# A spectral filter gated with a Mish layer: idle matmuls on a built-in f32 constant, and a weight load cut in two with a table between

## The chip, the cores and the metric

The kernel runs on one core of a Trainium2 chip. The metric is device time in microseconds (us). Before the change the median of three runs is 135.92 us (135.65 to 135.99). Engines are named as in the profile: PE (matmul) with PEld (its weight loads), DVE, ACT, POOL, and SP, which issues most DMAs.

## What is computed

Two branches work on arrays of 2048 rows of 512, in bf16, and a gate for each row mixes them. Branch A filters `x` in the 2-D Fourier domain; branch B is a layer with Mish and a second layer; both take the same `x` (`A_x`).

```python
g = sigmoid((x * gate_w).sum(-1, keepdims=True))          # x = A_x, [1, 2048, 512]
X = rfft2(x.astype(float32)) * (A_w_r + 1j * A_w_i)       # weights [2048, 257]
a = irfft2(X, s=(2048, 512)).astype(bfloat16)
h = einsum("bsd,df->bsf", x, B_w1) + B_b1                 # 512 -> 1792
b = einsum("bsf,fd->bsd", h * tanh(softplus(h)), B_w2)    # 1792 -> 512
return g * a + (1 - g) * b
```

## The kernel before

The rows are 16 tiles of 128 (`t`), in four chunks of four tiles (`c`). Everything is on one core, and PE does nearly all of it: both Fourier transforms are matmuls with tables of cosines and sines that the program holds as constants in DRAM.

**Branch B.** `x` is transposed on PE tile by tile (L516, with a permutation `pid` that POOL builds) and copied to `xT`. Layer 1 (L575, `layer1`) is, for a chunk and for each of 14 blocks `ft` of 128 columns of `w1`, four matmuls of 128x512 into one PSUM bank; ACT applies Mish with the bias (L560). Layer 2 (L903, L886) is 14 matmuls for each tile, scaled by one minus the gate at eviction.

**Branch A.** The transform along a row (L609 to L612, `a1`, with the table `FDs`), the transform along the columns in two steps (L630 and L745) with a trip through DRAM between, the filter on DVE and POOL (L756, L762), the way back (L798, a second trip through DRAM, L828 and L846), and the mix.

**The head.** The first chunk is taken in halves, so that PE can begin with part of the loads. Tiles 0 and 2 (`b`=0) and 1 and 3 (`b`=1) come in two loads of `x` (`ld_x0`), and the first 512 columns of `w1` in four loads, one for each block `dt_` of 128 input rows (`ld_w1d`). PE transposes tiles 0 and 2 (eight transposes, `tr0d0` to `tr0d3`); then `early0` to `early3` (L590) multiply them with one `ld_w1d` piece each, four matmuls of 256 columns, one for each of four output blocks; after `early0` come the eight transposes of tiles 1 and 3 (`tr1d*`). `late0` to `late3` (L590, four matmuls each) do the second half of the four blocks. The rest of chunk 0 (`mm1_0_4` on, L575) needs further loads of `w1`: `ld_w1(4, 8)` for blocks 4 to 7, `ld_w1(8, 14)` for the others. The row transforms need `FDs` (`ld_fd`).

**Idle matmuls.** Until the first load has landed, PE multiplies a tile of zeros with itself (`warm`, L504; `zt` is set by DVE at L500). The one piece of real work in between is the transpose of the bias (`tr_small`, L519). Their number is set by the planner.

**What sets the order.** The order on every engine is written by a planner when the program is built (`_Graph.schedule`, L215). Each task has an engine, a duration, dependencies and a priority. The planner walks through time, takes the ready task that can start first (within 0.1 us the one of highest priority), and books its duration. DMAs have an estimated bandwidth `bw`, from which the planner books when they land (L287 to L295); loads on one queue stay in the order in which they are written down. Idle matmuls are *fillers* of priority 1, which are dropped as soon as `early0` has been placed (L239). On the chip each engine runs its list in that order and waits on semaphores; the planner's times do not reach the chip, only the order.

SP's list begins: `x0` first half, `w1d0`, `x0` second half, `w1d1`, `w1d2`, `w1d3`, `w1` 4 to 7, `FDs`, `x` of chunk 1, `w1` 8 to 13, the table `m1`, `x` of chunks 2 and 3, and smaller ones. POOL issues the filter's weights and `w2` when `w1` 8 to 13 has landed.

Of the kernel before, what the change touches and what calls it, by code (L numbers as in the profile page):

```python
# [7 lines left out]
BF = mybir.dt.bfloat16  # L8
F32 = mybir.dt.float32
AF = mybir.ActivationFunctionType  # L10
# [20 lines left out]
def _bf16_bits(a):  # L31
    a = np.ascontiguousarray(a, dtype=np.float32)
    u = a.view(np.uint32)
    r = (u + np.uint32(0x7FFF) + ((u >> np.uint32(16)) & np.uint32(1))) >> np.uint32(16)
    return r.astype(np.uint16)
# [280 lines left out]
def _build(nc, A_x, A_w_r, A_w_i, B_x, B_w1, B_b1, B_w2, gate_w, out):  # L316
    cs = _build_consts()
    d_FD = nc.inline_tensor(_bf16_bits(cs["FD"]), name="c_fd").bitcast(BF)
# [7 lines left out]
    G = _Graph()  # L326
    es = ExitStack()
    with es:
        def sb(name, shape, dt):
            return es.enter_context(nc.sbuf_tensor(name, shape, dt))  # L330

        xo = sb("xo", [128, NT, 512], BF)
# [4 lines left out]
        act = sb("act", [128, 3, NFT, 512], BF)  # L337
        w1_sb = sb("w1_sb", [128, 4, F], BF)
        w2_sb = sb("w2_sb", [128, NFT, 512], BF)
        FDs = sb("FDs", [128, 768], BF)  # L340
# [6 lines left out]
        Ybuf = sb("Ybuf", [128, 32 * KR], BF)  # L347
        junk = sb("junk", [128, 512], BF)
        gwb = sb("gwb", [128, 512], BF)
        zt = sb("zt", [128, 256], BF)  # L350
        braw = sb("braw", [14, 128], BF)
        b1f = sb("b1f", [128, NFT], F32)
        gdot = sb("gdot", [128, NT], F32)
# [12 lines left out]
        q1 = sb("q1", [128, 2, 2, 16], F32)  # L366
# [25 lines left out]
        ps = es.enter_context(nc.psum_tensor("ps", [128, 8, 512], F32))  # L392
        psb = ps.bitcast(BF)

        xv = A_x[0].rearrange("(s p b) d -> p s b d", s=2, b=8)
        ov = out[0].rearrange("(s p b) d -> p s b d", s=2, b=8)
        w1v = B_w1.rearrange("(dt p) f -> p dt f", p=128)
# [7 lines left out]
        def new_sem(name):  # L405
            return es.enter_context(nc.semaphore(name))
# [5 lines left out]
        def dma(name, dst, src, reads=(), writes=(), nbytes=0, deps=(), is_out=False, prio=None, queue="sp", bw=300e3):  # L412
            dur = 1.0 if queue == "pool" else 0.5

            def fn(e, _dst=dst, _src=src):
                return e.dma_start(_dst, _src)

            t = G.add(name, queue, dur, fn, reads=reads, writes=writes, lat=2.0 + nbytes / bw, deps=deps, prio=prio)
            t.xfer = nbytes / bw
            t.isdma = True  # L420
            if is_out:
                t.sem = out_sem
                n_out_dma[0] += 1
                t.semval = 16 * n_out_dma[0]
            else:
                t.sem = new_sem("d_" + name)
                t.semval = 16
            return t
# [16 lines left out]
        def evict(name, n, dst, src, reads, writes, prio=None, rate=1.0):  # L445
# [9 lines left out]
              reads=["ones"], writes=["perm"])  # L455
        G.add("id14", "pool", 0.2, lambda e: e.affine_select(out=id14[:, :], in_=id14[:, :], pattern=[[1, 14]],
                                                             compare_op=ALU.is_equal, fill=0.0, base=0, channel_multiplier=-1),
              reads=["ones"], writes=["id14"])

        def ld_x(c, s0, s1):  # L460
            dma(f"ld_x{c}{s0}", xo[:, 4 * c + 2 * s0:4 * c + 2 * s1, :].rearrange("p (s b) d -> p s b d", b=2), xv[:, s0:s1, 2 * c:2 * c + 2, :],
                writes=[("x", t) for t in range(4 * c + 2 * s0, 4 * c + 2 * s1)], nbytes=128 * 2048 * (s1 - s0), bw=330e3 if c == 1 else 380e3)

        def ld_x0(b):
            dma(f"ld_x0{b}", xo[:, b:4:2, :], xv[:, :, b, :], writes=[("x", b), ("x", 2 + b)], nbytes=128 * 2048, bw=(218e3, 350e3)[b])

        def ld_w1d(dt_):
            dma(f"ld_w1d{dt_}", w1_sb[:, dt_, 0:512], w1v[:, dt_, 0:512], writes=[("w1d", dt_)], nbytes=128 * 1024, bw=350e3)

        def ld_w1(lo, hi):  # L470
            return dma(f"ld_w1_{lo}", w1_sb[:, :, 128 * lo:128 * hi], w1v[:, :, 128 * lo:128 * hi],
                       writes=[("w1", f) for f in range(lo, hi)], nbytes=512 * 256 * (hi - lo), bw=220e3 if lo == 4 else 380e3)

        dma("ld_b1", braw[:, :], B_b1.rearrange("(ft p) -> ft p", p=128), writes=["braw"], nbytes=3584, queue="act", prio=100.0)
        ld_x0(0)
        ld_w1d(0)
        ld_x0(1)
        for dt_ in range(1, 4):
            ld_w1d(dt_)
        ld_w1(4, 8)  # L480
        dma("ld_fd", FDs[:], d_FD[:], writes=["FD"], nbytes=128 * 1536, bw=262e3)
        ld_x(1, 0, 2)
        t_w1 = ld_w1(8, 14)
        dma("ld_m1", m1g1[:, 0:2048], d_M1.rearrange("p b h c m -> p (b h c m)"), writes=["m1"], nbytes=128 * 4096)
        ld_x(2, 0, 2)
# [4 lines left out]
        for i in range(2):  # L490
            for q in (0, 2, 1, 3):
                dma(f"ld_W{i}{q}", WT[32 * q:32 * q + 32, i, :, :].rearrange("p g k -> p (g k)"), Wv[i][q],
                    writes=[("W", i, q)], nbytes=32 * 8224, queue="pool", deps=[t_w1])
        WALL = [("W", i, q) for i in range(2) for q in range(4)]
        for h in range(2):
            dma(f"ld_w2_{h}", w2_sb[:, 7 * h:7 * (h + 1), :], w2v[:, 7 * h:7 * (h + 1), :],
                writes=[("w2", h)], nbytes=128 * 7 * 1024, queue="pool", deps=[t_w1])


        G.add("zero", "dve", 0.15, lambda e: e.memset(zt[:, :], 0.0), writes=["zt"], prio=99.0)  # L500
        G.add("table", "act", 1.5, lambda e: e.activation(q1[:, 0, 0, 0:1], zt[:, 0:1], AF.Mish), reads=["zt"], prio=99.0)
        for i in range(NWARM):
            n_ = 256 if i < 15 else 128
            G.add(f"warm{i}", "pe", n_ / 1200, lambda e, n_=n_: e.matmul(ps[:, 6, 0:n_], zt[:, 0:128], zt[:, 0:n_], start=True, stop=True),  # L504
               reads=["zt"], prio=1.0).filler = True


        SP0 = PR['sp0']
# [2 lines left out]
        def f_tr(e, ts, dts, at):  # L511
# [8 lines left out]
           reads=["braw", "id14"], writes=[("bank", 0)], prio=SP0 + 4.0)  # L520
        G.add("ev_small", "act", 0.25, lambda e: e.activation(b1f[:, :], psb[:, 0, 0:14], AF.Copy), reads=[("bank", 0)], writes=["b1f"], prio=SP0 + 1.05)
        for b in range(2):
            for dt_ in range(4):
                bk = (dt_ + 1) % 4
                pe(f"tr{b}d{dt_}", 2 * mm((256, 128)[b]), lambda e, dt_=dt_, bk=bk, b=b: f_tr(e, (b, 2 + b), (dt_,), lambda t, d_: (bk, t // 2)),
                   reads=[("x", b), ("x", 2 + b), "perm"], writes=[("bank", bk)], prio=SP0 + 1.0 + 2.5 * b - 0.01 * dt_)
# [3 lines left out]
                      reads=[("bank", bk)], writes=[("xT", t, dt_) for t in (b, 2 + b)], prio=SP0 + 1.1)  # L530

        for c in range(NCH):
            for t in range(4 * c, 4 * c + 4):
                if c > 0:
                    pe(f"tr{t}", 4 * mm(128), lambda e, t=t: f_tr(e, (t,), range(4), lambda t, dt_: (1, dt_)), reads=[("x", t), "perm"],
                       writes=[("bank", 1)], prio=SP0 + 1.0)
# [7 lines left out]
            for h, op in ((0, ALU.add), (1, ALU.subtract)):  # L544
# [3 lines left out]
                lo, hi = uv[:, 0:2, r2, :], uv[:, 2:4, r2, :]  # L548
# [45 lines left out]
        for dt_ in range(4):  # L594
            t_e = pe(f"early{dt_}", 4 * mm(256) * (1.8 if dt_ == 0 else 1), lambda e, dt_=dt_: f_early(e, range(4), (dt_,), 0), writes=[("bank", b) for b in EB],
                     reads=[("xT", 0, dt_), ("xT", 2, dt_), ("w1d", dt_)], prio=PR['mm1c0'] + 8)
            if dt_ == 0:
                G.filled = t_e
        for ft in range(4):
            pe(f"late{ft}", 4 * mm(256), lambda e, ft=ft: f_early(e, (ft,), range(4), 1), writes=[("bank", EB[ft])],  # L600
               reads=[("xT", t, dt_) for t in (1, 3) for dt_ in range(4)] + [("w1d", dt_) for dt_ in range(4)], prio=PR['mm1c0'] + 7 - 0.01 * ft)
            mish(0, ft, EB[ft])

        for t in range(NT):
            a1b = t % 2 if t >= 8 else 0

            def f_a1(e, t=t, a1b=a1b):
# [9 lines left out]
               writes=[("bank", a1b)], prio=SP0)  # L617
# [4 lines left out]
            if t % 4 == 3:  # L622
# [17 lines left out]
                for h in range(2):  # L640
                    t_r1w.append(dma(f"r1w{t}_{h}", scr1_w[h][:, b0:b0 + 8, :], Y1[64 * h:64 * h + 64, b0:b0 + 8, :],
                                     reads=[("Y1", b0 + i) for i in range(8)], writes=[("scr1", b0 + i, h) for i in range(8)],
                                     nbytes=64 * 8 * 512, prio=SP0 + 1.0, bw=180e3))
# [3 lines left out]
        for t in range(NT):  # L647
# [3 lines left out]
                  reads=[("x", t), "gw"], writes=[("gd", t), "junk"], deps=s1_tasks[2:3])  # L651
# [37 lines left out]
        for n in range(4):  # L689
            t_r1r.append(dma(f"r1r{n}", In2[:, :, 2 * n:2 * n + 2, :].rearrange("p q u k -> p q (u k)"), scr1_r[:, :, 512 * n:512 * n + 512],  # L690
                             reads=[("scr1", b, h) for b in range(32) for h in range(2)],
                             writes=[("In2", q, u) for q in range(4) for u in (2 * n, 2 * n + 1)],
# [43 lines left out]
        for n in range(4):  # L736
            zb = n % 2

            def f_s2(e, n=n):
                ins = None  # L740
                for c in range(2):
                    for q in range(4):
                        for h in range(2):
# [6 lines left out]
                               reads=[("In2", q, 2 * n + uu) for q in range(4) for uu in range(2)] + ["sm"], writes=BSB))  # L750
            for i in range(4):
                h, uu = divmod(i, 2)
                u, pb = 2 * (2 * n + uu) + h, uu
                for (nm, Pb, Wu) in (("1", P1b, WT[:, :, u, 0:256]), ("2", P2b, WT[:, ::-1, u, 0:256])):
# [5 lines left out]
                          reads=[("bank", 2 * h), ("bank", 2 * h + 1)] + WALL, writes=[("P" + nm, pb)])  # L760
                for (c, nm, Pb, op) in ((0, "1", P1b, ALU.subtract), (1, "2", P2b, ALU.add)):
# [3 lines left out]
                                reads=[("P" + nm, pb)], writes=[("Z", zb, i, c)])  # L765
                if n == 0 and i == 1:
                    s2_tasks.append(pe("s2x", 0.8, f_s2x, reads=[("In2", q, u_) for q in range(4) for u_ in range(8)] + ["sm", "rr"],
                                       writes=[("bank", 0), ("bank", 1)]))
# [4 lines left out]
                          reads=["q"], writes=["zr"])  # L773
                    G.add("zi", "pool", 0.15, lambda e: e.tensor_tensor(out=zi[:], in0=q2[:, 0], in1=q2[:, 1], op=ALU.add),
                          reads=["q"], writes=["zi"])
                    G.add("z0r", "pool", 0.15, lambda e: e.tensor_tensor(out=z0[:, 0, :], in0=zr[:, 0, :], in1=zi[:, 1, :], op=ALU.subtract),
                          reads=["zr", "zi"], writes=["z0r"])
                    G.add("z0i", "pool", 0.15, lambda e: e.tensor_tensor(out=z0[:, 1, :], in0=zi[:, 0, :], in1=zr[:, 1, :], op=ALU.add),
                          reads=["zr", "zi"], writes=["z0i"])
            if n == 0:  # L780
                G.add("gexp", "pool", 2.9, lambda e: e.tensor_tensor(out=gexp[:, :], in0=gbase[:, :], in1=gdot[:, :], op=ALU.pow),  # L781
                      reads=[("gd", t) for t in range(NT)] + ["gbase"], writes=["gexp"])
                G.add("gden", "pool", 0.2, lambda e: e.tensor_scalar(out=gexp[:, :], in0=gexp[:, :], scalar1=1.0, scalar2=None, op0=ALU.add),
                      reads=["gexp"], writes=["gden"])
                G.add("gcol", "dve", 0.2, lambda e: e.reciprocal(out=gcol[:, :], in_=gexp[:, :]), reads=["gden"], writes=["gcol"])
                G.add("omg", "dve", 0.1, lambda e: e.tensor_scalar(out=omg[:, :], in0=gcol[:, :], scalar1=-1.0, scalar2=1.0, op0=ALU.mult, op1=ALU.add),
                      reads=["gcol"], writes=["omg"])
            G.add(f"wc_{n}", "pool", 0.2, lambda e, n=n, zb=zb: e.tensor_copy(
                out=Zb[:, zb, :, :, :, 0], in_=z0[:].rearrange("p c (u h) -> p h c u", h=2)[:, :, :, 2 * n:2 * n + 2]),
                reads=["z0r", "z0i"], writes=[("Z", zb, 4)])  # L790

            def f_s2i(e, zb=zb):
# [10 lines left out]
               writes=BSB)  # L803
# [3 lines left out]
            for h in range(2):  # L807
                t_r2w.append(dma(f"r2w{n}{h}", scr2_w[h][:, :, 512 * n:512 * n + 512],
                                 T2s[64 * h:64 * h + 64, :, 2 * n:2 * n + 2, :].rearrange("p q u k -> p q (u k)"),
                                 reads=[("T2s", n, 0), ("T2s", n, 1)], writes=[("scr2", n, h)], nbytes=64 * 4096))  # L810
# [3 lines left out]
        for tq in range(8):  # L814
            b0 = 4 * tq
            dma(f"r2r{tq}", T2r[:, b0:b0 + 4, :], scr2_r[:, b0:b0 + 4, :],
                reads=[("scr2", n, h) for n in range(4) for h in range(2)], writes=[("T2r", b0 + i) for i in range(4)],
# [49 lines left out]
        for c in range(NCH):  # L867
# [7 lines left out]
            for tl in range(4):  # L875
                t = 4 * c + tl
                bank = 4 + (t % 2)
                if t == NT - 1:
                    G.cur_prio = PR['mm2'] - 10
                    for i, (c0, w_) in enumerate(((0, 384), (384, 128))):  # L880
                        cs_, bk = slice(c0, c0 + w_), 1 + i

                        def f_mm2h(e, t=t, tl=tl, bk=bk, hb=hb, cs_=cs_, w_=w_):
                            ins = None
                            for ft in range(NFT):
# [5 lines left out]
                           writes=[("bank", bk)])  # L891
# [3 lines left out]
                              reads=[("bank", bk), "omg", ("ga", t, 0), ("ga", t, 1), ("x", t)], writes=[("o", t, i)], prio=PR['fin'])  # L895
# [3 lines left out]
                for lo, hi in ((0, 4), (4, 7), (7, 11), (11, 14)):  # L899
                    def f_mm2(e, t=t, tl=tl, bank=bank, lo=lo, hi=hi, hb=hb):  # L900
# [7 lines left out]
                       reads=[("act", hb, ft) for ft in range(lo, hi)] + [("w2", lo // 7)], writes=[("bank", bank)])  # L908
                if t < NBF:
                    evict_b(t, bank)  # L910
                else:
# [3 lines left out]
                          reads=[("bank", bank), "omg", ("ga", t, 0), ("ga", t, 1)], writes=[("x", t), ("o", t)], prio=PR['fin'])  # L915
# [116 lines left out]
```

## Time and profile before

| | before |
|---|---|
| median of 3 runs | 135.92 us (135.65 to 135.99) |
| profiled execution | 135.63 us |
| its span, first to last instruction | 133.9 us |
| DVE's memset of `zt` (L500) | 0.89 to 1.06 |
| POOL's memsets of built-in constants (L1017) | 0.31 to 0.50 |
| issue on SP of the four pieces `w1d1` to `w1` 4-7 | 1.89 us |
| load of `w1` 4-7 (512 KB), issue to landing | 5.8 us |
| load of `FDs` (192 KB), issue to landing | 5.8 us |
| load of `x`, chunk 1 (512 KB), issue to landing | 7.0 us |
| ACT busy | 79.6 us (59%) |
| DVE busy | 88.9 us (66%) |

Times in the views count from the span's first instruction. An instruction is named by line, engine, operation and tiles (`ps<-zt` writes PSUM and reads `zt`), with partitions x elements and type, and `x9` is nine of them merged into one row. A matmul's own duration holds its way through the array's pipe, so what the array takes is read from the distance of starts. Some matmul records are missing from the trace: the first L575 row of the timeline has three matmuls at 10.31, and PEld shows four weight loads from 9.99.

### The profile page before, as it was taken

The page shows a single profiled execution, that of the slowest core. Times are in us where ns is not written, and L with a number is a line of the kernel's source. Part 1 is how long each engine was busy: PE and PEld are TensorE (multiplying, and loading weights), DVE is VectorE, ACT ScalarE, POOL GpSimd, SP SyncE. Part 2 cuts the span into 40 slices and gives each one's busy share as a digit, 9 for nine tenths or more (in the row PEclk, how much of TensorE's full clock was granted, in tenths as well). Part 3 has the DMA queues.
Part 4 walks back from the last instruction along what each step waited for, and adds up shares of the span by engine and source line. Part 5 has one row for each costly group of instructions (what it writes and reads, how often), then busy time and mean ns, then how long its engine had stood idle before and what let it go on. Part 6 is the DMA issues. An engine that isn't in the chain of part 4 may idle for free.

```text
span 133.9 us, 2695 instructions
## 1 busy us (share of the span) xinstructions
PE 128.9 (96%) x1030; PEld 69.5 (52%) x1047; DVE 88.9 (66%) x213; ACT 79.6 (59%) x130; POOL 27.4 (20%) x56
## 2 busy tenths in 40 slices
PE   6999999999999999999999999999999999999992
PEld 4885655655544443443443443443445877755452
DVE  0286298989689982963893893794001699999422
ACT  4258798899988786605256657434333789792000
POOL 2000793014000009583440440440000000000000
PEclk9999999999999999999999999999999999999999
DMA  3899999999262399450600600600649700305321
GB/s 114 238 294 367 397 284 299 288 366 344 62 157 58 99 293 334 98 220 0 157 5 0 157 2 0 156 6 0 157 150 277 204 2 0 130 32 215 113 102 42
DMA packets 18937, 20.82 MB, mean 155 GB/s; under 512 B 1196, under 2 KB 16172, under 8 KB 18540
## 3 DMA queue, kind: packets, MB, share of 16 engines
q1 hardware_dynamic: 17888, 16.67, 41.1%
q0 software_dynamic: 864, 3.94, 9.4%
q8 instruction: 8, 0.13, 0.4%
q10 hardware_dynamic: 172, 0.04, 0.1%
q14 instruction: 5, 0.04, 0.1%
HBM read 14.35 MB, written 6.29 MB: 154 GB/s over the span
## 4 chain that ended last, share of the span: by engine, by line
PE 90%; ACT 6%; issue 1%; DVE 0%
PE ps L903 34%; PE ps L575 31%; PE ps L846 5%; ACT act L560 3%; PE ps L828 3%; ACT Ybuf L447 3%; PE ps L504 2%; PE ps L516 2%; PE ps L886 2%; PE ps L612 2%; PE ps L590 2%; PE ps L798 2%; PE ps L745 2%; PE ps L630 1%; PE ps L609 1%
## 5 line engine op out<-in xcount | busy, mean ns | idle before, releaser
L575 PE MATMUL ps<-xT,w_sb 128*128 128x512 bf16 x199 | 48.1, 379 | 0.8 <-issue 0.2
L903 PE MATMUL ps<-w_sb,act 128*128 128x512 bf16 x202 | 46.9, 379 | 0.6 <-issue 0.3
L560 ACT ACTIVATE act<-ps,b1f 128x512 bf16<-128x512 f32 x56 | 37.8, 692 | 12.8 <-PE ps L575 10.9
L903 PEld LDWEIGHTS ps<-w_sb,act 128*128 128x128 bf16 x210 | 20.2, 98 | 23.2 <-issue 1.2
L575 PEld LDWEIGHTS ps<-xT,w_sb 128*128 128x128 bf16 x208 | 19.4, 98 | 22.3 <-issue 2.1
L756 DVE TENSOR_TENSOR misc<-ps,WT 128x512 f32<-128x512 f32 x32 | 19.8, 681 | 5.9 <-PE ps L745 5.9
L858 ACT ACTIVATE xo<-ps,omg 128x512 bf16<-128x512 f32 x12 | 8.3, 690 | 19.5 <-PE ps L903 18.9
L762 POOL TENSOR_TENSOR misc<-misc 128x255 bf16<-128x255 f32 x17 | 12.1, 732 | 18.4 <-DVE misc L756 18.4
L446 DVE CAST Ybuf<-ps 128x512 bf16<-128x512 f32 (+1 forms) x9 | 8.2, 926 | 9.1 <-PE ps L798 7.3
L850 ACT ACTIVATE misc<-ps,gcol 128x512 f32<-128x512 f32 x16 | 10.7, 692 | 2.5 <-PE ps L846 2.4
L853 DVE TENSOR_TENSOR Tg<-misc 128x256 bf16<-128x256 f32 x32 | 11.7, 419 | 0.6 <-ACT misc L850 0.5
L446 DVE CAST misc<-ps 128x512 bf16<-128x512 f32 x7 | 4.8, 687 | 10.5 <-PE ps L828 10.5
L447 ACT ACTIVATE Ybuf<-ps 128x512 bf16<-128x512 f32 (+1 forms) x15 | 9.9, 714 | 2.9 <-PE ps L798 2.8
L649 DVE SCALAR_TENSOR_TENSOR junk<-xo,gwb 128x512 bf16<-128x512 bf16 x16 | 11.0, 690 | 0.7
L846 PE MATMUL ps<-GDs,misc 128*128 128x256 bf16 x64 | 9.3, 273 | 0.0
L447 ACT ACTIVATE Abuf<-ps 128x512 bf16<-128x512 f32 x13 | 7.7, 604 | 0.0
L446 DVE COPY xT<-ps 128x512 bf16<-128x512 bf16 x10 | 4.2, 422 | 4.6 <-PE ps L516 4.5
L516 PEld LDWEIGHTS ps<-pid,xo 128*128 128x128 bf16 x64 | 5.6, 111 | 3.1 <-DVE xT L446 0.4
L846 PEld LDWEIGHTS ps<-GDs,misc 128*128 128x128 bf16 x64 | 6.0, 98 | 2.1
L516 PE MATMUL ps<-pid,xo 128*128 128x128 bf16 x64 | 6.8, 243 | 0.0
L781 POOL TENSOR_TENSOR gexp<-gbase,gdot 128x16 f32<-128x16 f32 x1 | 2.9, 2943 | 18.5 <-DVE junk L649 18.5
L612 PE MATMUL ps<-FDs,Tg 128*128 128x256 bf16 x32 | 6.0, 273 | 0.0
(85 smaller groups left out, 112.8 us busy)
## 6 DMA issues: line engine op xcount, KB each, us to landing
scr<-Ybuf SPq DMA_DIRECT2D x16, 256.0 KB, 3.9
Abuf<-scr SPq DMA_DIRECT2D x4, 512.0 KB, 5.8
Abuf<-scr SPq DMA_DIRECT2D x8, 256.0 KB, 4.9
w_sb<-in_B_w_dram POOLq DMA_DIRECT2D x2, 896.0 KB, 14.2
out_dram<-xo SPq DMA_DIRECT2D x7, 256.0 KB, 2.1
xo<-in_A_x_dram SPq DMA_DIRECT2D x3, 512.0 KB, 9.8
WT<-in_A_w_r_dram POOLq DMA_DIRECT2D x4, 257.0 KB, 9.1
WT<-in_A_w_i_dram POOLq DMA_DIRECT2D x4, 257.0 KB, 10.8
```

Of the source, the lines that this page charges most:

```text
L446: G.add_multi(name, [("dve", dve_dur(n, rate=rate), lambda e: e.tensor_copy(out=dst, in_=src)), ("act", act_dur(n), lambda e: e.activation ...
L447: ("act", act_dur(n), lambda e: e.activation(dst, src, AF.Copy))],
L516: ins = e.transpose(psb[:, bank, 128 * col:128 * col + 128], xo[:, t, 128 * dt_:128 * (dt_ + 1)], perm[:, :])
L560: lambda e: e.activation(act[:, c % 3, ft, :].rearrange("p (t a b) -> p t a b", t=4, b=4), ps[:, bank, :].rearrange("p (t b a) -> p t a b" ...
L575: ins = e.matmul(ps[:, bank, :], w1_sb[:, dt_, 128 * ft:128 * (ft + 1)], xT[:, dt_, 4 * c:4 * c + 4, :], start=(dt_ == 0), stop=(dt_ == 3))
L649: lambda e, t=t: e.scalar_tensor_tensor(out=junk[:, :], in0=xo[:, t, :], scalar=1.0, in1=gwb[:, :], op0=ALU.mult, op1=ALU.mult, accum_out= ...
L756: lambda e, Pb=Pb, Wu=Wu, h=h, uu=uu, pb=pb: e.tensor_tensor(out=Pb[:, pb, :].rearrange("p (c j m) -> p c j m", c=2, j=2), in0=ps[:, 2 * h ...
L762: fz = (lambda e, c=c, Pb=Pb, op=op, pb=pb, h=h, uu=uu, zb=zb: e.tensor_tensor(out=Zb[:, zb, h, c, uu, 1:256], in0=Pb[:, pb, 1:256], in1=P ...
L846: ins = e.matmul(ps[:, yk, 256 * (j // 2):256 * (j // 2) + 256], TT[:, ts_, j // 2, s1, j % 2, :], GDs[:, j, :], start=(j % 2 == 0), stop= ...
L850: G.add(f"geo_{t}", "act", act_dur(512, True), lambda e: e.activation(gEO[:, gb, :], ps[:, yk, :], AF.Copy, scale=gcol[:, t:t + 1]), reads ...
L853: fg = (lambda e, i=i, op=op: e.tensor_tensor(out=ga[:, t, 256 * i:256 * i + 256], in0=gEO[:, gb, 0:256], in1=gEO[:, gb, 256:512], op=op))
L903: ins = e.matmul(ps[:, bank, :], act[:, hb, ft, 128 * tl:128 * (tl + 1)], w2_sb[:, ft, :], start=(ft == 0), stop=(ft == NFT - 1))
```

## The change

The tile `zt` and its memset go. The idle matmuls read a constant 1.0 that the program's opening writes in any case, one f32 for each partition, read again and again by a stride of zero. Their weights are 32 columns, so they write 32 partitions of the bank, and they have 128 moving columns (the first eight) or 64. ACT's first activation, which loads the function table, reads the same constant.

The load of blocks 4 to 7 of `w1` is cut in two, blocks 4 and 5 and blocks 6 and 7, and the load of the row transform's table `FDs` stands between them. The planner's bandwidths of the first loads are changed, and the planner books `n_ / 600` for an idle matmul of `n_` columns instead of `n_ / 1200`.

```diff
-        zt = sb("zt", [128, 256], BF)
...
         def ld_x0(b):
-            dma(f"ld_x0{b}", xo[:, b:4:2, :], xv[:, :, b, :], writes=[("x", b), ("x", 2 + b)], nbytes=128 * 2048, bw=(218e3, 350e3)[b])
+            dma(f"ld_x0{b}", xo[:, b:4:2, :], xv[:, :, b, :], writes=[("x", b), ("x", 2 + b)], nbytes=128 * 2048, bw=(403e3, 262e3)[b])
...
         def ld_w1d(dt_):
-            dma(f"ld_w1d{dt_}", w1_sb[:, dt_, 0:512], w1v[:, dt_, 0:512], writes=[("w1d", dt_)], nbytes=128 * 1024, bw=350e3)
+            dma(f"ld_w1d{dt_}", w1_sb[:, dt_, 0:512], w1v[:, dt_, 0:512], writes=[("w1d", dt_)], nbytes=128 * 1024, bw=(187e3, 238e3, 291e3, 187e3)[dt_])
...
         def ld_w1(lo, hi):
...
-                       writes=[("w1", f) for f in range(lo, hi)], nbytes=512 * 256 * (hi - lo), bw=220e3 if lo == 4 else 380e3)
+                       writes=[("w1", f) for f in range(lo, hi)], nbytes=512 * 256 * (hi - lo), bw={4: 194e3, 6: 291e3}.get(lo, 380e3))
...
-        ld_w1(4, 8)
-        dma("ld_fd", FDs[:], d_FD[:], writes=["FD"], nbytes=128 * 1536, bw=262e3)
+        ld_w1(4, 6)
+        dma("ld_fd", FDs[:], d_FD[:], writes=["FD"], nbytes=128 * 1536, bw=115e3)
+        ld_w1(6, 8)
...
-        G.add("zero", "dve", 0.15, lambda e: e.memset(zt[:, :], 0.0), writes=["zt"], prio=99.0)
-        G.add("table", "act", 1.5, lambda e: e.activation(q1[:, 0, 0, 0:1], zt[:, 0:1], AF.Mish), reads=["zt"], prio=99.0)
+        ones = nc.const_aps.tensor(1.0, (128, 256))
+        G.add("table", "act", 1.5, lambda e: e.activation(q1[:, 0, 0, 0:1], ones[:, 0:1], AF.Mish), prio=99.0)
         for i in range(NWARM):
-            n_ = 256 if i < 15 else 128
-            G.add(f"warm{i}", "pe", n_ / 1200, lambda e, n_=n_: e.matmul(ps[:, 6, 0:n_], zt[:, 0:128], zt[:, 0:n_], start=True, stop=True),
-               reads=["zt"], prio=1.0).filler = True
+            n_ = 128 if i < 8 else 64
+            G.add(f"warm{i}", "pe", n_ / 600, lambda e, n_=n_: e.matmul(ps[0:32, 6, 0:n_], ones[:, 0:32], ones[:, 0:n_], start=True, stop=True),
+                  prio=1.0).filler = True
```

In the order that the planner writes, PE's list begins with 12 idle matmuls (8 of 128 columns, 4 of 64), the transpose of the bias and 5 of 64 columns, in place of 9, the transpose and 5 of 256. Then come the same transposes, early and late groups. Behind them the transform of tile 0 stands after the first L575 group as before, that of tile 1 now ahead of the transposes of tile 4, so those follow three L575 groups and two transforms instead of two groups and one. Further on, single groups of L575, L903 and L846 change places.

## The prediction

> **What bounds the kernel now.** The page first: how full PE is, and who holds the chain that ended last.
>
> ```profile
> span 133.9 us, 2695 instructions
> ...
> PE 128.9 (96%) x1030; PEld 69.5 (52%) x1047; DVE 88.9 (66%) x213; ACT 79.6 (59%) x130; POOL 27.4 (20%) x56
> ...
> PE 90%; ACT 6%; issue 1%; DVE 0%
> ```
>
> PE is busy for 96% of the span and makes 90% of the chain. A microsecond by which PE's stream comes later is a microsecond of the end, unless a wait behind it takes it up. The change lies in the first 10 us, so the second view is the timeline of that stretch (start, length in us, engine, line).
>
> ```profile
> 0.80 0.45 SPq L416 DMA_DIRECT2D xo<-in_A_x_dram  x1
> ...
> 1.11 2.10 PE L504 MATMUL ps<-zt 128*128 128x256 bf16 x9 [1.11 <-DVE zt L500]
> ...
> 3.15 0.19 PE L519 MATMUL ps<-pid,braw 14*128 14x14 bf16 x1
> ...
> 3.27 1.25 PE L504 MATMUL ps<-zt 128*128 128x256 bf16 x5
> ...
> 4.31 1.06 PE L516 MATMUL ps<-pid,xo 128*128 128x128 bf16 x8
> ...
> 5.16 1.06 PE L590 MATMUL ps<-xT,w_sb 128*128 128x256 bf16 x4
> ...
> 6.01 1.06 PE L516 MATMUL ps<-pid,xo 128*128 128x128 bf16 x8
> ...
> 6.87 3.40 PE L590 MATMUL ps<-xT,w_sb 128*128 128x256 bf16 x28
> ```
>
> Nine idle matmuls, the transpose of the bias, five more idle ones, then eight transposes of x, the first early group, eight transposes, and from 6.87 the three other early groups and the sixteen late matmuls. After 3.27 there is no hole. Starts give what the array takes: eight transposes of 128 columns 0.85 (0.107 each), four matmuls of 256 columns 0.85 (0.213 each).
>
> Third, the same matmul in two windows, 5.2 to 5.9 and 7.6 to 9.9 (busy us, mean ns of one, idle before).
>
> ```profile
> L590 PE MATMUL ps<-xT,w_sb 128*128 128x256 bf16 x4 | 1.1, 421 | 0.0
> ```
>
> ```profile
> L590 PE MATMUL ps<-xT,w_sb 128*128 128x256 bf16 x24 | 2.8, 273 | 0.0
> ```
>
> The clock row of the page shows full speed throughout, but the durations do not: one shape falls from 421 to 273 ns. In the window 6.86 to 7.25 two of them have a mean of 382, in the next one all have 273. From there four matmuls of 256 columns take 0.44 in the chain (0.109 each) and four transposes 0.22 (0.056 each): half. So PE starts at half rate and turns to full rate at about 7.2. The last row's end, 10.27, less the pipe of its last matmul (0.273 - 0.109) puts PE through the head at **10.10**, the mark that I compare.
>
> Fourth, the loads of the head, one by one (size, us from issue to landing). The first half of x, issued at 0.80, lands after 2.7, at 3.5; the first piece of w1 at 4.7, the other half of x at 5.4, the next pieces at 6.0 and 6.4, and the last of the four, issued at 3.26, at 7.5:
>
> ```profile
> w_sb<-in_B_w_dram SPq DMA_DIRECT2D x1, 128.0 KB, 4.3
> ```
>
> So at 4.31 the transposes wait for idle matmuls, not for x: 0.8 us lie there for the change to take. Behind them the last piece of w1 leaves only 0.3: the fourth early group needs it and runs at about 7.8.
>
> **The change, part by part.**
>
> *Start.* DVE's memset (0.89 to 1.06) and PE's wait for it go. The built-in constant is written by POOL at 0.34, ahead of the opening barrier, behind which SP issues at 0.80. PE then starts at about 0.83 instead of 1.11. ACT's table load needs the constant alone too; its first work for others is at 3.37, so that is worth nothing.
>
> *Idle matmuls.* Seventeen instead of fourteen: eight of 128 columns and four of 64, the bias transpose, five of 64. The operand is f32, and the program has two weight loads and two matmuls for each of them. No f32 matmul is in the trace, so bounds. From below: each of the two costs as a bf16 matmul of as many columns, 0.107 for 128 at half rate, so 0.213 for the pair. From above: a row of 128 f32 is as many bytes as the 256 bf16 of the old idle matmul, 0.213, so 0.427 for the pair. I take the upper one: the pair exists because a number twice as wide is taken in halves, and the moving operand is twice as wide too; by its bytes the nearest row is the old idle matmul itself. Both ends stay in the range. The weight load of 32 columns is hidden behind the matmul ahead of it, as loads of 128 columns (0.15 at most) are now.
>
> By the Trainium skill's page "FP8 and Floating Point Precision", section "TensorE Precision Notes", true FP32 takes four passes through the array. By it the sum would be that of the upper end, and it speaks against this change; no run here shows it yet.
>
> *The sum at 0.427, turn at 7.2.* Start 0.83; eight of 0.427 (3.41) and four of 0.213 (0.85): 5.10. Bias transpose 0.12 (3.15 to 3.27 now): 5.22. Five of 0.213: 6.28. Eight transposes: 7.14. First early group: 0.08 at half rate, the other nine tenths of it at full rate, 0.39: 7.61. Eight transposes 0.45: 8.06. Three early groups 1.31: 9.37; all loads have landed by then. Sixteen late ones 1.75: 11.12. That is **1.02 later** than 10.10. The cover that the old idle matmuls had (x lands at 3.5) is overrun by 2.8 us.
>
> *The second piece of w1 in two, the table between.* One more issue on SP's queue, 0.47 (four take 1.89 there), so everything from the second piece on is issued that much later. But those loads wait in the queue for 7 to 9 us, so a later issue hides. The bytes ahead of x's next load, of the rest of w1 and of the second table are the same. The runs are half as long (512 bytes). From below that costs nothing; from above the 512 KB take twice as long: they land at 9.6, 2.1 after the piece ahead, so 2.1 more for all behind. x's next load then lands at 13.9 instead of 11.8; in the new order its transposes come after three layer-1 groups (0.86) and two transforms (0.33), at 14.4. The rest of w1 would land at 16.1 and be used at 16.3. So nothing is late, by little; in rival 2 below, whose stream is 1.2 ahead, that end would hold PE for up to 0.8. The DFT table lands at 10.1 now and is used at 10.96; an earlier landing frees nothing, as PE is not through the head before.
>
> *Order.* The planner, given other landing times, puts the first two transforms a group earlier and swaps single groups later. The window from 9 to 30:
>
> ```profile
> 9.00:30.00 21.00, 20.56 (x215) 12.62 (x217) 15.94 (x42) 18.73 (x34) 7.34 (x14) 1.00 1.04 332
> ```
>
> PE idles 0.44 of 21 there, and ACT is busy for 18.73, so a swap can bring back 0.4 at most, or cost about as much where an eviction falls behind a Mish. I take 0.1 of cost.
>
> *Sum.* 135.63 (the profiled execution; span 133.87 and 1.76 around it) + 1.02 + 0.1 = 136.75. The median of the runs, 135.92, is 0.29 above the profiled one; for a typical execution that is **137.0** (+0.8%). Behind the head PE is the chain, so I let nothing of it be taken up.
>
> **Rivals.**
>
> *1. Not slower: the clock turns sooner.* In before, PE's loads stop for 0.41 ahead of the bias transpose, and the turn comes 3.95 after 3.27, where work runs on without a hole. If it is the hole that decides, a stream without a hole from 0.83 turns at 4.78. Half of the overrun then runs at full rate: idle matmuls end at 5.53, transposes 5.98, first early group 6.42, transposes 6.87, groups 7.31, 7.74, 8.18, late ones 9.93: 0.17 sooner than now. It needs idle matmuls that fill the wait for the bias at 3.15, which the 0.427 gives. Against it: one turn in one trace is no rule. Time: 135.8 with the 0.1.
>
> The Trainium skill's page "TensorE: Matmul & The Clock Gate", Part 1, says that full rate follows a busy window of about 3.4 us, and that windows run on freely. By it the turn is at 3.8, one window ahead of 7.2, if the earlier start fills that window enough, and the head then ends 0.35 sooner, held by the last piece of w1; before's turn, 6.1 after PE's first matmul, fits two such windows of which the first was not full.
>
> *2. No change: 0.213 for a pair.* The first twelve end at 2.96, the bias transpose still waits to 3.15, the other five end at 3.80; transposes 4.65, first group (its w1 lands at 4.7) 5.59, transposes 6.45, second group 7.27, then 7.70, 8.14, and the late ones 9.89. That is 0.2 sooner, 0.1 with the order: 135.8. For it: no row shows that a wider number costs array time. Against it: two matmuls, and twice the bytes in each.
>
> *3. Worse: the turn comes 3.4 later, at 10.6.* It decides if work on 32 of the 128 columns, or the small holes of rival 2, do not count as work for the clock. Then with 0.427 the head ends at 12.8 (138.6), and with 0.213 at 11.5 (137.4). Against it: the 14-row transpose and the waits before 3.27 are all the evidence there is.
>
> **How the numbers follow.** Forecast 0.36, rival 1 0.16, rival 2 0.29, rival 3 0.14 (half of it at either price), the rest 0.05. About 0.3% (0.4 us) is what a measurement of this kernel can tell from no change. Rivals 1 and 2 lie at 0.1 to 0.2 under the median, mostly within that; with the spread of the runs (135.65 to 135.99) and an order that may gain, a third of each falls on the faster side. Faster 0.17, same 0.29, slower 0.54 (the forecast, rival 3 and a little of rival 2). The range takes in rivals 1 and 2 with the order's gain (135.5) and the cheaper half of rival 3 with 0.7 for loads and order (138.1); the dear half is left out.
>
> **What would show it.** Right: f32 matmuls of L504 starting 0.21 apart (two for each idle matmul of 128 columns), the first transposes of x at about 6.3 with x long landed, L590's duration falling at about 7.2, PE through the head at 11.1, and the same stream 1 us later from there. Rival 1: durations fall before 5. Rival 2: starts 0.107 apart and transposes at 3.8. Rival 3: L590 at 421 ns to the end of the head. Wrong altogether: an L575 row behind the head that waits for a load, or the end moving by less than half of the head.

## The result, and the profile after

The changed kernel takes 136.52 us (median of 22 runs, 135.57 to 137.16), the kernel before 135.63 (22 runs, 135.26 to 136.39): a ratio of 1.0054, 95% interval 1.0035 to 1.0074. So it is slower, by 0.7 us as the ratio has it and by 0.9 between the medians. Ratios and intervals here go by fast runs alone, so a slow run each of e3 and e5 stands in the median but not in the ratio. The profiled execution took 136.41 us for a span of 134.7, 0.8 more than before's.

The page of the changed kernel, as above for before: PE is a little fuller and holds a little more of the chain (a part of which is that more matmul records are missing from before's trace).

```profile
span 134.7 us, 2753 instructions
...
PE 131.3 (97%) x1067; PEld 70.5 (52%) x1067; DVE 90.2 (67%) x214; ACT 78.5 (58%) x128; POOL 28.0 (21%) x56
...
PE 93%; ACT 5%; DVE 0%; issue 0%
```

The timeline of its head on PE (start, length in us):

```profile
0.83 4.44 PE L504 MATMUL ps<-const-float32-1.0 128*32 128x128 f32 x24 [0.83 <-PEq L1017]
5.21 0.19 PE L519 MATMUL ps<-pid,braw 14*128 14x14 bf16 x1
5.33 0.82 PE L504 MATMUL ps<-const-float32-1.0 128*32 128x64 f32 x10
6.09 0.62 PE L516 MATMUL ps<-pid,xo 128*128 128x128 bf16 x8
6.76 0.61 PE L590 MATMUL ps<-xT,w_sb 128*128 128x256 bf16 x4
7.21 0.61 PE L516 MATMUL ps<-pid,xo 128*128 128x128 bf16 x8
7.65 3.22 PE L590 MATMUL ps<-xT,w_sb 128*128 128x256 bf16 x28
10.71 1.03 PE L575 MATMUL ps<-xT,w_sb 128*128 128x512 bf16 x4
```

The first row holds twelve idle matmuls as 24 instructions (16 of 128 columns, 8 of 64). The wide ones fill 0.83 to 4.22: 0.213 each, 0.427 for a pair. The planner had booked 128 / 600 = 0.213 for the pair, half of that: at its price the whole fill would have ended at about 3.6. The transposes of x begin at 6.09 in place of 4.31, though the first half of x lands at 3.6. PE is through the head at 10.71, 0.61 later than before.

The forms of L504 in the window 0 to 9 (busy us, mean ns of one): the 64-column ones have a mixed mean, since they run in both states of the clock; L590 is all at full rate.

```profile
L504 PE MATMUL ps<-const-float32-1.0 128*32 128x128 f32 x16 | 3.6, 419 | 0.8 <-PEq L1017 0.8
L590 PE MATMUL ps<-xT,w_sb 128*128 128x256 bf16 x17 | 2.2, 273 | 0.1
L504 PE MATMUL ps<-const-float32-1.0 128*32 128x64 f32 x18 | 1.9, 268 | 0.0
```

An f32 matmul of 128 columns lasts 419 ns, what bf16 of 256 columns lasted at half rate. The trace also keeps a record of the clock, which lists the stretches at full and at half rate. It puts the turn to full rate at **5.50** here and at 7.22 in before.

### The profile page after: what moved, and what is told of

It is laid out like the page before. It is cut to its first block, busy times and chain, and to the rows that moved or that the text cites. A ratio compares the mean times of both kernels' runs of the same rounds, so it can differ in the third digit from the quotient of the medians.

```text
span 134.7 us, 2753 instructions
## 1 busy us (share of the span) xinstructions
PE 131.3 (97%) x1067; PEld 70.5 (52%) x1067; DVE 90.2 (67%) x214; ACT 78.5 (58%) x128; POOL 28.0 (21%) x56
## 4 chain that ended last, share of the span: by engine, by line
PE 93%; ACT 5%; DVE 0%; issue 0%
PE ps L903 34%; PE ps L575 32%; PE ps L846 5%; PE ps L504 4%; PE ps L590 3%; PE ps L828 3%; ACT Ybuf L446 3%; PE ps L886 2%; PE ps L612 2%; PE ps L798 2%; PE ps L516 2%; PE ps L745 2%; ACT act L560 1%; PE ps L630 1%; PE ps L609 1%; PE ps L610 1%
## 5 line engine op out<-in xcount | busy, mean ns | idle before, releaser
L575 PE MATMUL ps<-xT,w_sb 128*128 128x512 bf16 x208 | 49.7, 380 | 0.1
L903 PE MATMUL ps<-w_sb,act 128*128 128x512 bf16 x210 | 48.6, 380 | 0.0
L903 PEld LDWEIGHTS ps<-w_sb,act 128*128 128x128 bf16 x210 | 20.0, 98 | 23.1 <-issue 1.7
L575 PEld LDWEIGHTS ps<-xT,w_sb 128*128 128x128 bf16 x208 | 19.2, 98 | 22.2 <-ACT act L560 2.2
L445 DVE CAST misc<-ps 128x512 bf16<-128x512 f32 x8 | 5.4, 684 | 10.3 <-PE ps L828 10.3
L846 PE MATMUL ps<-GDs,misc 128*128 128x256 bf16 x64 | 9.1, 273 | 0.0
L846 PEld LDWEIGHTS ps<-GDs,misc 128*128 128x128 bf16 x64 | 6.0, 98 | 2.3
L446 ACT ACTIVATE Abuf<-ps 128x512 bf16<-128x512 f32 x12 | 7.1, 605 | 0.0
L516 PEld LDWEIGHTS ps<-pid,xo 128*128 128x128 bf16 x64 | 4.7, 98 | 3.0 <-DVE xT L445 0.4
L504 PE MATMUL ps<-const-float32-1.0 128*32 128x64 f32 (+1 forms) x34 | 5.3, 339 | 0.8 <-PEq L1017 0.8
```

What stands on the lines that cost most here:

```text
L445: G.add_multi(name, [("dve", dve_dur(n, rate=rate), lambda e: e.tensor_copy(out=dst, in_=src)), ("act", act_dur(n), lambda e: e.activation ...
L446: ("act", act_dur(n), lambda e: e.activation(dst, src, AF.Copy))],
L504: G.add(f"warm{i}", "pe", n_ / 600, lambda e, n_=n_: e.matmul(ps[0:32, 6, 0:n_], ones[:, 0:32], ones[:, 0:n_], start=True, stop=True), pri ...
L575: ins = e.matmul(ps[:, bank, :], w1_sb[:, dt_, 128 * ft:128 * (ft + 1)], xT[:, dt_, 4 * c:4 * c + 4, :], start=(dt_ == 0), stop=(dt_ == 3))
L846: ins = e.matmul(ps[:, yk, 256 * (j // 2):256 * (j // 2) + 256], TT[:, ts_, j // 2, s1, j % 2, :], GDs[:, j, :], start=(j % 2 == 0), stop= ...
L903: ins = e.matmul(ps[:, bank, :], act[:, hb, ft, 128 * tl:128 * (tl + 1)], w2_sb[:, ft, :], start=(ft == 0), stop=(ft == NFT - 1))
```

## The experiments

Three theories. *1*: the idle matmuls overrun the landing of x, because an f32 column costs twice a bf16 one in each of two matmuls. *2*, its rival: the cut load and the new order cost the time. *3*: the turn of the clock lies on a grid of its own, and makes the scatter of the runs.

Four numbers were read for each profile: the turn, by the clock record; PE's end of the head (the start of the last L590 plus 0.109); the span; and the span less the head's end, what is behind the head. Most runs have one profile each, so a row is one execution, while the times in the sections are of many.

| run | turn | end of head | span | behind the head |
|---|---|---|---|---|
| before | 7.22 | 10.10 | 133.87 | 123.77 |
| r4, before again | 5.20 | 9.98 | 133.69 | 123.71 |
| e1, f32 idle matmuls alone | 6.66 | 11.20 | 134.94 | 123.74 |
| e2, cut load alone | 4.84 | 9.30 | 134.37 | 125.07 |
| e6, bf16 constant, old loads and order | 3.68 | 9.97 | 133.71 | 123.74 |
| changed | 5.50 | 10.71 | 134.67 | 123.96 |
| r1, changed again | 4.15 | 10.17 | 134.06 | 123.89 |
| r2, changed again | 4.05 | 10.13 | 134.06 | 123.93 |
| r3, changed again | 4.36 | 10.27 | 134.22 | 123.95 |
| e3, bf16 constant, new loads and order | 4.49 | 9.39 | 133.31 | 123.92 |
| e4, no idle matmuls | 7.19 | 9.85 | 133.78 | 123.93 |
| e5, half the f32 columns | 4.50 | 8.94 | 132.94 | 124.00 |
| e7, as e3 with the load whole | 5.39 | 9.74 | 133.64 | 123.90 |
| e8, first half of x late, another order | 4.72 | 13.41 | 137.26 | 123.85 |

### e1: the new idle matmuls alone

Before, with the fill of the changed kernel; the orders of all engines are before's.

```diff
-NWARM = 60
+NWARM = 17
...
-            n_ = 256 if i < 15 else 128
-            ... matmul(ps[:, 6, 0:n_], zt[:, 0:128], zt[:, 0:n_], ...)
+            n_ = 128 if i < 8 else 64
+            ... matmul(ps[0:32, 6, 0:n_], ones[:, 0:32], ones[:, 0:n_], ...)
```

> The kernel before with the new idle matmuls alone (17 on the f32 constant with weights of 32 columns, as in the changed kernel); loads and every other order as before. Theory 1 (the idle matmuls overrun the landing of x; an idle matmul of 128 columns takes 0.427): the first transposes of x at 6.1 to 6.3, the time 0.6 to 1.0 us above before, about that of the changed kernel. Theory 2 (the cut load and the new order cost the time): within 0.2 us of before. Theory 3 (the clock turns on a grid of its own, wherever the kernel begins): the time scatters by over 1 us from run to run, and the turn in the profile is anywhere between 4.2 and 7.7.

136.14 us against 135.61: 1.0044, interval 1.0021 to 1.0067. The narrow idle matmuls and the transposes on PE:

```profile
5.33 1.28 PE L503 MATMUL ps<-const-float32-1.0 128*32 128x64 f32 x10
6.54 0.66 PE L515 MATMUL ps<-pid,xo 128*128 128x128 bf16 x8
```

The transposes come at 6.54, later than the 6.1 to 6.3 that were expected, because the turn came at 6.66 and the whole fill ran at half rate. The head ends at 11.20, the rest is as in before (123.74). Most of the change's cost is in this edit: 0.6 us by the ratio, of 0.7.

### e2: the cut load alone

```diff
-        ld_w1(4, 8)
+        ld_w1(4, 6)
         dma("ld_fd", ...)
+        ld_w1(6, 8)
```

The planner's bandwidths are set so that the orders stay.

> The kernel before with the second piece of w1 cut in two and the table between, and nothing else: idle matmuls and the order on PE, ACT, DVE and POOL as before. Theory 1: within 0.2 us of before, since x of chunk 1 lands at about 12.6 (as in the changed kernel) and its transposes come at 12.2 in this order, so at most some 0.4 us of wait. Theory 2: slower by 0.4 or more.

136.01 against 135.61: 1.0018, interval 0.9995 to 1.0040, not told from no change by its time, and between what the two theories expected. The profile is clearer. The waits of PE's weight loads in the window 9 to 14:

```profile
PEld ps L517 <- DMA xo<-in_A_x_dram: 1.6, 1, 1.6
```

The turn was early (4.84), the head ended at 9.30, and the transposes of chunk 1 then stood until x landed at 12.6. In the window 4.8 to 5.1 of before, and 5.3 to 5.7 of the changed kernel, the same load (us from issue, behind the size):

```profile
xo<-in_A_x_dram SPq DMA_DIRECT2D x1, 512.0 KB, 7.0
```

```profile
xo<-in_A_x_dram SPq DMA_DIRECT2D x1, 512.0 KB, 7.3
```

Issued 0.5 later and 0.3 longer under way (0.4 in e2 itself), it lands at 12.6 in place of 11.8. In the old order this takes back what an early end of the head gives (behind the head: 125.07); in the changed kernel the transposes come at 14.05 and do not wait for it.

### e3: a bf16 constant

The changed kernel, same constant in bf16; 256 and 128 columns, so that the planner books the same times and the order stays.

```diff
-        ones = nc.const_aps.tensor(1.0, (128, 256))
+        ones = nc.const_aps.tensor(1.0, (128, 256), BF)
-            n_ = 128 if i < 8 else 64
+            n_ = 256 if i < 8 else 128
```

> The changed kernel with the idle matmuls on the built-in bf16 constant, 256 and 128 columns in place of 128 and 64, weights of 32 columns; all orders as in the changed kernel. Theory 1: an idle matmul of 256 columns takes 0.213, the twelve end at 3.0, the transposes of x start at 3.8, the head ends 0.2 to 0.4 before that of the kernel before, and the time is 0 to 0.3 below before. Theory 2: 0.6 to 1.0 above before, as the changed kernel.

135.37 against 135.61: 0.9974, interval 0.9956 to 0.9992. With another type in the idle matmuls, and twice the columns, the change is a small gain. Theory 2 falls as the cause of the loss: the new loads and order are all in this kernel. The head on PE:

```profile
0.83 2.29 PE L504 MATMUL ps<-const-bfloat16-1.0 128*32 128x256 bf16 x12 [0.83 <-PEq L1017]
3.52 0.19 PE L519 MATMUL ps<-pid,braw 14*128 14x14 bf16 x1 [0.39 <-DMA braw<-in_B_b_dram]
3.64 0.71 PE L504 MATMUL ps<-const-bfloat16-1.0 128*32 128x128 bf16 x5
4.29 0.70 PE L516 MATMUL ps<-pid,xo 128*128 128x128 bf16 x8
```

Twelve idle matmuls end at 3.0 and PE waits for the bias, which came late in this run, as x did (4.1).

### e4: no idle matmuls

```diff
-NWARM = 60
+NWARM = 0
```

> The changed kernel without idle matmuls, all else the same. The transposes start when x has landed, at 3.6. If idle matmuls count as work for the clock (32 of 128 columns or not), the turn comes later than in the changed kernel, at 7.0 to 10.4 by a window of 3.4 us that must be full, and the head, half of it or all at half rate, ends at 10.2 to 11.8: 0 to 1.2 us above before, mean 0.6. If they do not count, the turn is where it is with them, and the time is below that of the changed kernel by the overrun, 0.9 us.

136.38 against 135.61: 1.0025, interval 0.9995 to 1.0056, not told apart; the runs scatter from 135.23 to 136.84. In the profile the turn is at 7.19: the window before it, 0.37 to 3.78, was all but empty, and the next one full. So the idle matmuls do count as work for the clock, as the turn at 7.0 or later was to show. The times span 1.61 us, as wide as the 1.59 of the changed kernel with its fill; the two were not run side by side, so whether the f32 fill is worth anything is not shown.

### e5: half the f32 columns

The changed kernel with 64 and 32 columns; the planner books `n_ / 300`, so the order stays.

> The changed kernel with 64 and 32 columns in its f32 idle matmuls in place of 128 and 64, nothing else. Theory 1 (the f32 columns alone make the loss: two matmuls of twice the array time for each column): idle matmuls of 64 columns start 0.107 apart, two for each, the fill ends near 3.8, and the time is that of the bf16 constant, 0.1 to 0.4 below before. If the weights of 32 columns or the f32 pair had a cost of their own beside the columns, the fill would end later than 4.2 at half rate.

135.42 against 135.39: 0.9984, interval 0.9956 to 1.0012. The transposes begin at 3.87, and 64 columns start 0.107 apart. So the columns set the price: neither the weights of 32 columns nor the pair has a fixed cost that shows. The time is between no change and e3's gain, and the interval does not tell which.

### e6: a bf16 constant in the old order

The kernel before, with ten idle matmuls of 256 columns and four of 128 on the bf16 constant.

> The kernel before with its idle matmuls on the built-in bf16 constant, starting at 0.83 and ending near 3.7 (10 of 256 columns, then 4 of 128); loads and order as before. If the new order is worth something because it puts the transposes of chunk 1 behind more work: here they wait for x of chunk 1 (11.8) whenever the head ends before 9.75, so the gain is 0 to 0.2 us, less than that of the bf16 constant in the new order. If the order is worth nothing or costs: 0.3 to 0.5 below before.

135.33 against 135.39: 0.9988, interval 0.9971 to 1.0006. The turn was the earliest of all (3.68), and still the head ended at 9.97: PE's weight loads stood for the pieces of w1, of which the fourth came at 7.7. What an earlier start can give is bounded there, in a profile with the load whole. The wait for chunk 1 that was expected did not come in this run, as the head was not early enough.

### e7: the load whole, in the new order

The kernel of e3 with blocks 4 to 7 of `w1` in one load ahead of the table; the planner's bandwidths are set so that the order stays.

> The bf16 constant in the changed kernel's order, with the second piece of w1 whole and the table behind it, as before. If the cut costs by landing x of chunk 1 later (12.6 in place of 11.8): those transposes come at 12.3 or later in this order, so with the cut they wait at times, and without it the time is up to 0.3 us below that of the bf16 constant with the cut. If the cut is hidden altogether: within 0.15 of it. If the earlier table is worth something: above it.

135.24 against 135.39: 0.9983, interval 0.9964 to 1.0002. Behind the head 123.90 against 123.92 in e3: with the new order the cut costs and gives nothing there.

Ahead of the head's end that is less clear. PE's weight loads in e7:

```profile
PEld ps L589 <- DMA w_sb<-in_B_w_dram: 0.7, 1, 0.7
```

In e3, e5, e6, e7 and r4 PE waits for the fourth piece of `w1`, and in all five the head ends 2.24 after that piece has landed (7.15, 6.70, 7.73, 7.50 and 7.74): there the load sets the head's end, and not the turn. With the load behind it whole the piece lands at 7.50 to 7.74 in four of five profiles (6.51 in e1), with the load cut at 6.33 to 7.15 in seven of eight (7.64 in r3; e8 apart). So the cut may bring this piece sooner. Why, and whether it is worth time, no run shows: e3's and e7's times do not differ clearly.

### e8: all real work behind the turn

The kernel of e3 with the first half of x loaded behind blocks 4 and 5 of `w1`, and 35 idle matmuls of 256 columns. The planner lays out another order.

> A probe of the spread: the bf16 constant with the first half of x loaded behind the first piece of w1 4-7, so that real work begins at 8.0 to 9.0, and idle matmuls (35 of 256 columns) up to there. The planner lays out another order for it, so its mean says nothing. Theory 3 (the turn falls anywhere in 4.2 to 7.7, and that makes the spread): all real work then runs at full rate in every run, and the spread of the 12 runs falls to 0.5 us or less (1.6 in the changed kernel). If the spread comes from loads or elsewhere: 1 us or more, as now.

138.86, in four runs only (138.67 to 139.28). A spread of 0.6 in four runs, where at most 0.5 in twelve was expected, settles nothing. In the profile PE stood 1.9 for x, so the landing of x sets the start of real work there; how that scatters one profile cannot show.

### r1 to r4: the same kernels again

> The changed kernel once more, for a second pair of turn and time. Theory 3 (the grid of the clock lies anywhere; all else in this head is fixed, since the loads have landed): with the turn at T, PE is through the head at 10.71 + 0.46 x (T - 5.50), T anywhere in 3.6 to 7.0, and the span is that plus 123.96 within 0.2. If the scatter comes from the loads or the tail: the span does not follow the turn.

> As the run before it: head end 10.71 + 0.46 x (T - 5.50), span 123.96 more, within 0.2.

> As the two runs before it: head end 10.71 + 0.46 x (T - 5.50), span 123.96 more, within 0.2.

> The kernel before once more, for its own pair. Theory 3: turn anywhere in 3.9 to 7.3; head end 10.10 at 7.22, earlier by half of what the turn is earlier, but not before 9.2 (the fourth piece of w1 at 6.7 to 7.5 and the work behind it); if the head ends before 9.75, PE waits for x of chunk 1 (11.8), so that the span does not fall below 133.5.

The three turns are 4.15, 4.05 and 4.36. Expected head ends are 10.09, 10.04 and 10.19, measured 10.17, 10.13 and 10.27; expected spans 134.05, 134.00 and 134.15, measured 134.06, 134.06 and 134.22. So in the changed kernel the time follows the turn, by these four profiles and e1's (r1 to r3 were taken on another chip than e1, and their turns lie close together). The measured ends of the head move by 0.39 to 0.42 for each us of the turn, a little less than the 0.46 expected: that makes 1.3 to 1.4 us for turns that differ by one window, 3.41, and the 22 runs spread over 1.59. That all of this spread is the turn's is not shown. In the kernel before the head does not follow it so: the second profile, with the turn 2.0 earlier, is only 0.18 shorter, as PE's weight loads waited 0.9 for the fourth piece of w1. The head was expected at 9.2 or a little later and ended at 9.98.

```profile
PEld ps L590 <- DMA w_sb<-in_B_w_dram: 0.9, 1, 0.9
```

What is behind the head groups by order: 123.71 to 123.77 in the old one (e2 apart), 123.89 to 124.00 in the new one. So the new order costs about 0.2 (0.12 to 0.29 between single profiles). The waits of PE's weight loads behind the head (11 to 60) point to where: in the changed kernel six times for a Mish to free a bank,

```profile
PEld ps L575 <- ACT act L560: 1.8, 6, 0.4
```

against 0.9 in three waits in before (9 to 60; the same from 11 on).

```profile
PEld ps L575 <- ACT act L560: 0.9, 3, 0.3
```

The count goes with the order: 1.8 in six waits in e3, e4, e5 and e7 too, 0.9 in three in e2 and e6. That these waits make the cost is not tested.

## Why the prediction was right, step by step

- *PE starts at 0.83*: 0.83.
- *An f32 pair of 128 columns takes 0.427*: 0.427, the upper of the two bounds. Rival 2 (0.213) falls. The Trainium skill's page "FP8 and Floating Point Precision", section "TensorE Precision Notes", with its four passes, agrees: two matmuls of 0.213 for 128 columns, against 0.107 for bf16.
- *The turn at 7.2*: the step that failed. It was carried over from one trace as if it belonged to the kernel. It was at 5.50, and at 4.05 to 6.66 in the other four profiles with this fill. With 5.50 in its place the prediction's own sum ends the head at 10.32 (a narrow f32 matmul at full rate taken at its measured 0.058), 0.22 late and not 1.02: 0.80 of the delay was too much.
- *No wait between the parts of PE's stream*: wrong as well, the other way. The head ended at 10.71, 0.61 late, so 0.39 were missing from the sum. PE's starts show 0.14 between the fill and the bias transpose, 0.10 between the fill and the transposes of x, and 0.22 for the copy of the first transposes, which the sum has at nothing. (The first counts about half, since the fill that it delays runs behind the turn.) The copy was hidden in before, where the transposes ran at half rate. The same sum with e1's turn of 6.66 gives 10.86, against 11.20 measured, so there too it is short. Two errors of opposite sign partly cancel, and that is luck. The wait for the copy in the changed kernel:

```profile
6.75 0.33 PEld L590 LDWEIGHTS ps<-xT,w_sb 128*128 128x128 bf16 x4 [0.22 <-DVE xT L529]
```

- *Order 0.1*: 0.19 by the two profiled executions (123.96 less 123.77). So 135.63 + 0.61 + 0.19 = 136.43, measured 136.41; this adds up the same two profiles and is no test of its own.
- *0.29 for a typical execution*: not there. Three runs had a median of 135.92; 22 have 135.63. The forecast less this and the 0.80 of the turn, plus the 0.39 of the waits and 0.09 of the order, is 136.4; measured 136.52.
- *The cut is hidden*: yes, in the new order. x of chunk 1 lands at 12.6, between the bounds of 11.8 and 13.9, and its transposes do not wait.
- *Rival 1, the hole decides*: falls. e3 turned at 4.49, 1.0 after its hole, and e1 at 6.66 with no hole from 0.84 up to 5. But an early turn, its sign, did come in r1 to r3 (4.05 to 4.36), with times of 135.79 to 135.95 where it had 135.8. Its other form, windows on a grid, is what the traces show. In all profiles full rate lasts for 126.29, 129.71 or 133.12 us: 37, 38 or 39 times 3.413. The Trainium skill's page "TensorE: Matmul & The Clock Gate", Part 1, gives windows of 3.413 us that run on freely, and the trace agrees. By that page the forecast should have been a mean over where the grid lies; the rival took the one grid of before.
- *Rival 3, 32 columns do not count as work*: falls. The window before the turn in the changed kernel holds idle matmuls for all but 0.2 us, and PE is busy for all of it:

```profile
2.09:5.50 3.41, 3.41 (x22) 2.86 (x21) 0.00 (x0) 0.96 (x3) 0.00 (x0) 1.00 0.90 291
```

The sign, the mechanism and its place were right: f32 idle matmuls at 0.427 overrun the landing of x. The size of the head's delay was wrong in two terms, of which the turn is the larger.

## What to carry to other kernels

Filler work must be priced by the type it reads: f32 cost four times the array time of bf16 for a column, and a fill that was planned at half of its price overran the load by 2.5 us. Ask of each filler what the first real work waits for, the load or the filler. Where the head of a kernel runs through the clock's turn, one profile shows one draw: compare the head's end together with the turn, and the work behind the head by itself. An early turn is worth only what the loads behind it allow.

## What was not expected of the hardware

How full a window must be: before's window from 0.39 to 3.80 had PE busy for 2.69 of 3.41 (79%, with the modelled ends of matmuls) and no turn followed; e6's from 0.27 to 3.68 had 2.85 (83%), and the clock turned at its end.

```profile
0.39:3.80 3.41, 2.69 (x13) 1.70 (x14) 0.17 (x1) 1.67 (x3) 0.85 (x8) 1.00 0.49 149
```

```profile
0.27:3.68 3.41, 2.85 (x15) 1.78 (x15) 0.00 (x0) 1.67 (x3) 0.93 (x8) 1.00 0.47 158
```

That is one window on each side. The idle matmuls of before read zeros and those of e6 ones, so that the data may count too stays open; no run tells them apart.
